# Turning stages 4 to 7 of an RWKV front by DMA instead of by matmul, with the first stages listed in a new order

## The chip, the cores and the metric

The kernel runs on one core of a Trainium2 chip. The metric is the device time of one execution in microseconds (us), as the median of several runs. The engines are called PE (TensorE: matmuls, and beside it PEld, its weight loads), DVE (VectorE), ACT (ScalarE), POOL (GpSimd) and SP (SyncE). POOL also issues the loads that change the number type on the way, SP the plain transfers and the DMA transposes.

## The reference

For batch `b` (4), head `h` (8), and tokens `t` (768) with head size D = 48, a linear attention with a decay per channel is computed, and its output of 3072 tokens by 384 channels goes through a two-layer MLP with a leaky ReLU:

```
for t in range(S):
    cur = einsum('bhd,bhe->bhde', u * k_t, v_t)
    y_t = einsum('bhd,bhde->bhe', r_t, state + cur)
    state = w * state + einsum('bhd,bhe->bhde', k_t, v_t)
...
h = x @ w_in                      # 384 -> 2048
out = maximum(0.01 * h, h) @ w_out   # 2048 -> 384
```

`r`, `k`, `v` and the weights arrive as float32 and are worked on in bfloat16.

## The kernel before, in words

The tokens are cut into 24 **stages** of 128 tokens; stage `n` is chunk `n // 4` of batch `n % 4`. Within a stage the recurrence is a masked product: r is scaled by `w^(t-64)` (table `qtab`), k by `w^(63-t)` (table `ktab`); both scaled tiles are turned, so that channels lie on partitions; their product (128 by 128 tokens for each head) is masked below the diagonal; it multiplies v, and the state carried from the stage four before is added. The diagonal term with `u` comes for stages 0 to 7 (`DIAG`) as a scaled v, and for later stages as a diagonal tile that POOL writes ahead of the mask. The MLP takes the stage's output (`xT`) through `w_in` (four column groups) and `w_out`.

All the instructions are recorded in one list by a small scheduler (`Sched`), which keeps for every buffer its writer and readers and puts semaphore waits where another engine or a transfer is involved. Each engine executes its own instructions strictly in the order of the record, so the order is all that decides who stands behind whom. There are eight PSUM banks, handed out in the order of the record: `take` gives the bank that has been free longest, and the matmul that gets it waits for the last reader of its former content.

The record has two parts. The front (stages 0 to 7, and parts of stages 8 to 13) is written out by hand as a string of steps, `ORDER`; behind it a loop over pairs of stages (`for m in range(FIRST // 2, ...)`) makes the rest by rule. The loop is the same in both kernels. The first step of its first turn, called J3 in the prediction, is eight pairs of `w_in` products for stages 6 and 7 (48 matmuls, line 628).

A step in `ORDER` is a letter and a stage. Those that matter here:

- `k4`, `r4`, `v4`: load of one stage's k, r or v with a cast from float32 to bfloat16 (1024 rows of 48 numbers), issued by POOL (line 223). `k0` and `r0` are plain loads from ACT and SP. `wi2`: one of four groups of `w_in` (line 233). `wo2`: one of four of `w_out` (line 237).
- `P4q`, `P4k`: DVE scales r or k of stage 4 into `qk` (line 353).
- `T4q`, `T4k`: four matmuls with the identity turn it into PSUM (line 407); `t4q`, `t4k`: ACT copies that into `tp` (line 421), or DVE does where an `@` follows (line 419).
- `X8T`: SP issues one DMA transpose that turns r and k of a stage together, from `qk` to `tp` (line 358). `X4` without a `T`: DVE's product of both turned tiles (line 368), for the diagonal term of stages 0 to 7.
- `A`: the eight matmuls of the masked product, into two banks (line 432). `Ma`, `Mb`: DVE masks one bank (line 441, from stage 8 on line 445). `D`: four small matmuls for the diagonal term (line 460). `Q`: the scaled v on DVE (line 375), from stage 8 on two diagonal tiles on POOL (line 393). `q8`: the row sums that these need, three DVE instructions (lines 382 to 386), which read `u_tab`.
- `Y`: the output of a stage on PE (lines 559 and 566), `y`: ACT copies it to `xT` (line 580). `K`: k times v on PE (line 473), `S`: the new state on DVE (line 531, from stage 4 on 534 and 536).
- `G0.2`: 12 matmuls of stage 0 with `w_in` group 2 (line 605), `g0.2`: ACT's leaky ReLU of it (line 615). `J2.5`: six matmuls of twice the width for stages 4 and 5 (line 628), `j2.5` its leaky ReLU (line 638). `H0`: 16 matmuls with `w_out` (line 652), `h0`: ACT's copy and SP's output transfer (lines 664 and 666).
- `F12`: 12 matmuls on ones with no use for their result (line 261), called fillings. `tri`, `id`: mask and identity on POOL. `bc`, `lnw`, `qtab`, `ktab`: the decay tables.
- `u`, `u16`, `U`, `utab`: u is loaded as one row, cast by ACT, spread over the partitions by a matmul with ones, and copied to `u_tab` by ACT (lines 676, 326, 330, 335).

`TURNED` names the first stage that isn't turned by matmul; the front's steps are written to agree with it.

Of the kernel before, what the change touches and what calls it, by code (L numbers as in the profile page):

```python
# [7 lines left out]
AF = mybir.ActivationFunctionType  # L8
AX = mybir.AxisListType
BF16 = mybir.dt.bfloat16  # L10
FP32 = mybir.dt.float32
# [6 lines left out]
HD = H * D  # L18
# [4 lines left out]
NSL = HD // 128  # L23

FIRST, NB, PACE = 6, B, 3
TURNED, DIAG, CARRY, EXACT = 8, 8, 4, 1
ORDER = """
w k0 r0 w8 u8 u wlz tcol k1 ones table one exps qk0 r1 v0z r5 F12 bc wi2 lnw id qtab wu8 v0 id8 u16 F13 Cm P0q ktab U
k3 P1q T0q Wl P0k utab T1q r3 P1k t0q T0k C P5q W T1k t1q@ k4 T5q t0k t1k@ tri t5q F2 A0 X0 v1 X1 F2 A1 M0a F3 D0 wi1
M0b F5 D1 F1 K0 k5 P3k P3q F11 T3k Q0 r4 F3 T3q P4k t3k F3 Y0 M1b v3 t3q T4k M1a y0 F2 K1 A3 r2 t4k Q1 F1 G0.2 M3a wi3  # L30
F1 Y1 S1 g0.2 G0.1 M3b v5 y1 X3 F2 G1.2 r7 P5k g0.1 S0 T5k g1.2 D3 P4q k6 G1.1 Q3 t5k T4q r6 g1.1 K3 P2q Y3 S3 t4q T2q
k2 X5 y3 F2 A5 X4 F1 A4 t2q M5a G3.2 v4 M4b F1 G3.3 wi0 g3.2 M4a D4 D5 G0.3 g3.3 k7 M5b G1.3 P7q g0.3 v7 Q5 K5 P6k G3.1
g1.3 S5 wo2 T6k g3.1 Y5 P6q v2 P2k t6k T6q Q4 y5 r10 F2 K4 T2k t6q@ T7q t2k Y4 v6 t7q@ A6 y4 S4 F1 A2 wo3 G1.0 M6a r11
F1 J2.7 P7k g1.0 M6b wo0 J2.0 j2.7 M2b J2.6 v8 j2.0 X2 M2a J2.2 j2.6 wo1 K7 J2.1 j2.2 v9 S7 K2 J2.4 j2.1 S2 r9 G0.0
P10q j2.4 r8 K6 J2.3 g0.0 S6 v11 D2 G3.0 j2.3 X6 Q2 k8 T7k g3.0 D6 J2.5 Q6 t7k k11 Y2 P11q j2.5 X7 A7 k9 y2 Y6 M7a k10
D7 M7b y6 G2.1 Q7 v10 G2.0 g2.1 G2.3 g2.0 G2.2 g2.3 H1 g2.2 P9q P8q H2 h1 P8k q8 X8T K8 H0 h2 P9k Q8 S8 X9T P10k P11k
K9 X10T H3 h0 q9 X11T S9 Q9 Y7 h3 A9 y7 A8 M8a M9a M9b M8b k12 r12 v12 k13 r13 v13
"""


# [4 lines left out]
class Sched:  # L45
# [7 lines left out]

    def add(self, eng, emit, R=(), W=(), dma=None):
        o = Op()
        o.eng, o.emit, o.dma, o.inc, o.val = eng, emit, dma, False, None
        deps = []
        for key in R:
            w = self.writer.get(key)
            if w is not None:  # L60
                deps.append((w, True))
        for key in W:
            w = self.writer.get(key)
            if w is not None:
                deps.append((w, False))
            for r in self.readers.get(key, ()):
                deps.append((r, False))
        o.deps = []
        for d, raw in deps:
            if d.dma is None and d.eng == eng and dma is None and (eng == "pe" or not raw):  # L70
                continue
            if d is not o and d not in o.deps:
                o.deps.append(d)
        for key in R:
            self.readers.setdefault(key, []).append(o)
        for key in W:
            self.writer[key] = o
            self.readers[key] = []
        self.ops.append(o)
        return o  # L80
# [47 lines left out]
def bass_rwkv5_eagle__then__act_leaky_relu_kernel(  # L128
# [13 lines left out]
    def SB(name, shape, dt=BF16):  # L142
        return ctx.enter_context(nc.sbuf_tensor(name, shape, dt))
# [5 lines left out]
    k_sb = SB("k_sb", [128, NST, HD])  # L149
    v_sb = SB("v_sb", [128, NST, H * E])  # L150
    w_row = SB("w_row", [128, HD // 2], FP32)
    u_row = SB("u_row", [1, HD], FP32)
    one_row = SB("one_row", [128, 128], FP32)
    u_row16 = SB("u_row16", [1, HD])
    w_head = SB("w_head", [H, D], FP32)
    u_head = SB("u_head", [H, D], FP32)
    wu_head = SB("wu_head", [H, D], FP32)
# [3 lines left out]
    lnw = SB("lnw", [128, HD], FP32)  # L161
    u_tab = SB("u_tab", [128, HD])
    k_f = SB("k_f", [128, EXACT, HD], FP32)
    r_f = SB("r_f", [128, EXACT, HD], FP32)
    qtab = SB("qtab", [128, HD])
    ktab = SB("ktab", [128, HD])
    tcol = SB("tcol", [128, 1], FP32)
# [4 lines left out]
    ones = SB("ones", [128, 128])  # L172
# [17 lines left out]
    V, A, PE, SP, G = nc.vector, nc.scalar, nc.tensor, nc.sync, nc.gpsimd  # L190
    sch = Sched(ctx, nc)
    add = sch.add
    free = list(range(8))

    def take():
        i = free.pop(0)
        return ps[i], ("ps", i)

    def give(key):
        free.append(key[1])  # L200

    def dram(h, offset, pattern):
        return bass.AP(tensor=h.tensor, offset=h.offset + offset, ap=pattern)
# [12 lines left out]
    def load_one(n, which, pace=()):  # L216
# [4 lines left out]
        else:  # L221
            dst = {"k": k_sb, "r": r_sb}[which][:, n, :].rearrange("p (h d) -> p h d", d=D)
        add("pool", lambda: G.dma_start(dst, src), R=pace, W=[(which, n)], dma=f"{which}{n}")  # L223

# [12 lines left out]
        add("pool", lambda: G.dma_start(w_out_sb[:, 4 * i:4 * i + 4, :], wout_view[:, 4 * i:4 * i + 4, :]),  # L237
            W=[("wout", i)], dma=f"wout{i}")

    def row(h):  # L240
        return dram(h, 0, [[HD, 1], [1, HD]])

    def by_head(h):
        return dram(h, 0, [[D, H], [1, D]])
# [11 lines left out]
    def fill(n):  # L256
# [6 lines left out]

        add("pe", emit, R=["ones"], W=[("ps", i), f"fill{n}"])

    def identity():
        add("pool", lambda: G.affine_select(ident[:, :], ones[:, 0:128], pattern=[[1, 128]], compare_op=ALU.is_equal,
                                            fill=0.0, base=0, channel_multiplier=-1), R=["ones"], W=["ident"])

# [52 lines left out]
        add("dve", lambda: V.tensor_tensor(wu_head[:, :], w_head[:, :], u_head[:, :], ALU.mult),  # L322
            R=["w_head", "u_head"], W=["wu_head"])

    def u_cast():
        add("act", lambda: A.activation(u_row16[:, :], u_row[:, :], AF.Copy), R=["u_row"], W=["u_row16"])

    def u_spread():
        ps_u, key = u_bank["u"] = take()
        add("pe", lambda: PE.matmul(ps_u[:, 0:HD], ones[0:1, 0:128], u_row16[:, :], start=True, stop=True),  # L330
            R=["ones", "u_row16"], W=[key])

    def u_table():
        ps_u, key = u_bank["u"]
        add("act", lambda: A.activation(u_tab[:, :], ps_u[:, 0:HD], AF.Copy), R=[key], W=["u_tab"])
        give(key)

    u_bank, c_bank = {}, {}
    at_bank, kv_bank, y_bank = {}, {}, {}

    def hd(x):
# [316 lines left out]
    def g2_out(n, c0=0, c1=HD):  # L658
# [14 lines left out]
            W=["w_row"], dma="w"),  # L673
        "w8": lambda: add("sp", lambda: SP.dma_start(w_head[:, :], by_head(w)), W=["w_head"], dma="w8"),
        "u8": lambda: add("sp", lambda: SP.dma_start(u_head[:, :], by_head(u)), W=["u_head"], dma="u8"),
        "u": lambda: add("sp", lambda: SP.dma_start(u_row[:, :], row(u)), W=["u_row"], dma="u"),
        "one": lambda: add("dve", lambda: V.memset(one_row[:, :], 1.0), W=["one_row"]),
        "tcol": tokens, "ones": filled, "exps": exponents, "v0z": zero_v, "qk0": zero_qk, "wlz": zero_w,
        "id": identity, "tri": triangle, "table": preload, "id8": small_identity, "wu8": wu_product,
        "bc": spread_w, "lnw": log_w, "qtab": lambda: table(qtab, qexp, "q"), "ktab": lambda: table(ktab, kexp, "k"),  # L680
        "Cm": columns_mm, "Wl": log_columns, "C": decay_columns, "W": decay_table,
        "u16": u_cast, "U": u_spread, "utab": u_table,
    }
    stage = {
        "P": lambda n, x: prep_half(n, half_of[x]), "T": lambda n, x: turn_mm(n, half_of[x]),
# [108 lines left out]
```

## Time and profile before

| what | before |
|---|---|
| median of 3 runs | 172.35 us (171.53 to 172.49) |
| span of the profiled execution | 168.6 us |
| granted clock of PE | 1.00 of full speed in every stretch |
| PE, DVE, ACT, POOL busy | 163.7, 106.9, 90.8, 103.6 us |
| matmuls | 2170 |
| fillings (line 261) | 69 matmuls |
| DMA transposes | 16, median 2.8 us from issue to landing |

The span runs from the first to the last instruction of the profiled execution; the profile gives no device time of its own for that execution, so the median of the runs stands beside the span, 3.75 us above it. In the views a row has the line of the kernel, the engine, the operation, the tiles (out<-in) and a count; times are us from the span's start. A chain of waits goes back from the last instruction, at each step to what released it.

### The profile page before, as it was taken

The numbers are of one execution on the slowest core, as the hardware profiler recorded it, in microseconds if no ns is written. First come the engines' busy times: TensorE is split into PE (matmuls) and PEld (weight loads), VectorE is DVE, ScalarE is ACT, GpSimd is POOL, SyncE is SP. The second block draws the span as 40 slices with busy tenths as digits, with TensorE's granted clock in tenths as the row PEclk, the third lists the DMA queues.
The fourth block names the chain that finished last, engine by engine and source line by source line (L and its number), as shares of the span: only waits on it lengthen the run. The fifth ranks groups of instructions, "written<-read, shape, count | busy, mean of one in ns | idle before, by whom it ended". The sixth has DMA issues, their size and how long they took to land.

```text
span 168.6 us, 5011 instructions
## 1 busy us (share of the span) xinstructions
PE 163.7 (97%) x2170; PEld 126.1 (75%) x2170; DVE 106.9 (63%) x217; ACT 90.8 (54%) x167; POOL 103.6 (61%) x117
## 2 busy tenths in 40 slices
PE   6899999999999999999999999999999999999994
PEld 4787898988667867867867867768768668668663
DVE  6599799874583999869959959969876050000000
ACT  3837866886123933933834735735637538449221
POOL 7999999990249998994993993993708100000000
PEclk9999999999999999999999999999999999999999
DMA  6999999999999959999599399299241011011012
GB/s 99 142 151 165 170 167 173 182 184 148 130 167 187 163 75 144 155 118 173 71 140 167 64 141 177 71 132 193 59 121 47 0 51 47 0 51 47 29 68 95
DMA packets 99148, 19.67 MB, mean 117 GB/s; under 512 B 92339, under 2 KB 99126, under 8 KB 99126
## 3 DMA queue, kind: packets, MB, share of 16 engines
q0 software_dynamic: 76512, 10.03, 92.1%
q1 hardware_dynamic: 21574, 9.12, 23.2%
q8 instruction: 17, 0.28, 0.7%
q10 hardware_dynamic: 1040, 0.20, 0.6%
q14 instruction: 5, 0.04, 0.1%
HBM read 20.45 MB, written 4.72 MB: 149 GB/s over the span
## 4 chain that ended last, share of the span: by engine, by line
PE 89%; POOL 5%; DMA 4%; issue 0%; ACT 0%; POOLq 0%
PE ps L652 37%; PE ps L628 31%; PE ps L605 6%; PE ps L566 6%; DMA w_in_sb<-in_moe_w_in_dram 4%; PE ps L432 4%; PE ps L473 2%; POOL k_sb L223 2%; POOL r_sb L223 2%; PE ps L407 1%; POOL v_sb L223 1%; PE ps L559 1%; PE ps L261 0%; POOL w_in_sb L233 0%; PE ps L460 0%
## 5 line engine op out<-in xcount | busy, mean ns | idle before, releaser
L652 PE MATMUL ps<-w_out_sb,gT 128*128 128x384 bf16 (+2 forms) x400 | 65.7, 320 | 0.0
L628 PE MATMUL ps<-xT,w_in_sb 128*128 128x256 bf16 x480 | 54.7, 273 | 0.0
L652 PEld LDWEIGHTS ps<-w_out_sb,gT 128*128 128x128 bf16 x400 | 37.9, 98 | 22.0
L393 POOL TENSOR_TENSOR at<-ident,s_tok 128x512 bf16<-128x512 bf16 x32 | 35.0, 1121 | 26.9 <-DVE s_tok L386 26.9
L628 PEld LDWEIGHTS ps<-xT,w_in_sb 128*128 128x128 bf16 x480 | 46.6, 98 | 6.4 <-ACT xT L580 0.2
L638 ACT ACTIVATE gT<-ps 128x512 bf16<-128x512 f32 x80 | 47.8, 597 | 6.4 <-PE ps L628 1.6
L664 ACT ACTIVATE out_sb<-ps 128x384 f32<-128x384 f32 (+2 forms) x25 | 11.9, 478 | 52.9 <-PE ps L652 52.9
L445 DVE CAST_PREDICATED at<-mask,ps 128x512 bf16<-128x512 uint16 x32 | 19.8, 684 | 18.0 <-PE ps L432 18.0
L223 POOL DMA_DIRECT2D v_sb<-in_v_dram x24 | 22.9, 955 | 0.0
L223 POOL DMA_DIRECT2D k_sb<-in_k_dram x23 | 21.5, 965 | 0.4 <-issue 0.4
L223 POOL DMA_DIRECT2D r_sb<-in_r_dram x23 | 21.2, 930 | 0.0
L353 DVE TENSOR_TENSOR qk<-r_sb,qtab 128x384 bf16<-128x384 bf16 x23 | 14.2, 617 | 3.8 <-DMA r_sb<-in_r_dram 3.8
L353 DVE TENSOR_TENSOR qk<-k_sb,ktab 128x384 bf16<-128x384 bf16 x23 | 13.0, 570 | 1.3 <-DMA k_sb<-in_k_dram 1.3
L580 ACT ACTIVATE xT<-ps 128x384 bf16<-128x384 f32 x24 | 11.0, 491 | 4.8 <-PE ps L566 4.8
L605 PE MATMUL ps<-xT,w_in_sb 128*128 128x128 bf16 x192 | 12.5, 219 | 0.4 <-DMA w_in_sb<-in_moe_w_in_dram 0.4
L615 ACT ACTIVATE gT<-ps 128x512 bf16<-128x512 f32 x16 | 9.6, 597 | 5.3 <-PE ps L605 4.9
L605 PEld LDWEIGHTS ps<-xT,w_in_sb 128*128 128x128 bf16 x192 | 11.0, 98 | 0.8 <-DMA w_in_sb<-in_moe_w_in_dram 0.5
L384 DVE TENSOR_TENSOR rku<-r_sb,ku 128x384 bf16<-128x384 bf16 x16 | 10.8, 675 | 0.6
L566 PE MATMUL ps<-at,v_sb 128*32 128x128 bf16 x384 | 10.8, 220 | 0.0
L534 DVE TENSOR_TENSOR sum_t<-ps,st 128x384 bf16<-128x384 f32 x16 | 8.8, 551 | 2.7 <-PE ps L473 2.7
L441 DVE TENSOR_TENSOR at<-ps,mask 128x512 bf16<-128x512 f32 x16 | 10.3, 681 | 0.3 <-PE ps L432 0.3
L261 PE MATMUL ps<-ones 128*128 128x128 bf16 x69 | 8.5, 257 | 1.3 <-DVE ones L251 1.3
(60 smaller groups left out, 135.1 us busy)
## 6 DMA issues: line engine op xcount, KB each, us to landing
out_dram<-out_sb SPq DMA_DIRECT2D x23, 192.0 KB, 3.6
v_sb<-in_v_dram POOLq DMA_DIRECT2D x24, 96.0 KB, 6.3
k_sb<-in_k_dram POOLq DMA_DIRECT2D x23, 96.0 KB, 6.1
r_sb<-in_r_dram POOLq DMA_DIRECT2D x23, 96.0 KB, 5.9
w_in_sb<-in_moe_w_in_dram POOLq DMA_DIRECT2D x4, 384.0 KB, 6.8
w_out_sb<-in_moe_w_out_dram POOLq DMA_DIRECT2D x4, 384.0 KB, 9.3
tp<-qk SPq DMA_TRANSPOSE x16, 2.8
k_f<-in_k_dram ACTq DMA_DIRECT2D x1, 192.0 KB, 2.7
```

The source lines that it names most:

```text
L223: add("pool", lambda: G.dma_start(dst, src), R=pace, W=[(which, n)], dma=f"{which}{n}")
L353: add("dve", lambda: V.tensor_tensor(qk[iq][:, H * half:H * half + H, 0:D], hd(src), hd(tab[:, :]), ALU.mult), R=[(name, n), "qk"[half] + ...
L384: add("dve", lambda: V.tensor_tensor(rku[i2][:, :], r_of(n), ku[i2][:, :], ALU.mult), R=[("r", n), ("ku", i2)], W=[("rku", i2)])
L393: add("pool", lambda hh=hh, s_of=s_of: G.tensor_tensor(at[ia][:, hh, :, :], ident[:, :].unsqueeze(1).to_broadcast([128, NP, 128]), s_of.un ...
L445: add("dve", lambda: V.copy_predicated(at[n % NAT][:, hh, :, :], mask[:, :].bitcast(mybir.dt.uint16).unsqueeze(1).to_broadcast([128, NP, 1 ...
L566: last = PE.matmul(ps_y[32 * q:32 * q + 32, 128 * s:128 * s + 128], a, m, start=not whole and step == 0, stop=step == len(columns[q]) - 1)
L580: add("act", lambda: A.activation(xT[m % NX][:, :, 128 * half:128 * half + 128], ps_y[:, 0:HD].rearrange("p (s t) -> p s t", t=128), AF.Copy),
L605: last = PE.matmul(ps_g[:, 128 * f:128 * f + 128], w_in_sb[:, s, 128 * fb:128 * fb + 128], xT[ix][:, s, t], start=s == 0, stop=s == NSL - 1)
L628: last = PE.matmul(ps_g[:, 256 * f:256 * f + 256], w_in_sb[:, s, 128 * fb:128 * fb + 128], xT[ix][:, s, :], start=s == 0, stop=s == NSL - 1)
L638: add("act", lambda: A.activation(gT[ig][:, 2 * j:2 * j + 2, :].rearrange("p f t -> p (f t)"), ps_g[:, :], AF.Prelu, alpha=0.01), R=[key], ...
L652: last = PE.matmul(ps_o[:, 0:c1 - c0], gT[ig][:, s, 128 * half:128 * half + 128], w_out_sb[:, s, c0:c1], start=s == 0, stop=s == NFB - 1)
L664: add("act", lambda: A.activation(out_sb[io][:, c0:c1], ps_o[:, 0:c1 - c0], AF.Copy), R=[key], W=held)
```

## The change

Stages 4 to 7 are turned by DMA transposes as the later ones were (`X4T` to `X7T`), so their `T` and `t` steps are gone: 32 matmuls, six evictions on ACT and two on DVE. `u_tab` is filled by one casting transfer on POOL's queue that reads the row of u for each of the 128 partitions; the row tile, its cast, its matmul and its eviction are gone. The whole string `ORDER` is new: the order of the loads, of the first stages' steps on every engine, and the places and lengths of the fillings (F15, F8, F12, F16, F26, 77 in all, against 69). The number of products, masks and MLP matmuls is the same. `k12`, `r12`, `v12` and `r13` now stand ahead of POOL's diagonal tiles `Q8` and `Q9`, and `v13`, `k13` and `v11` between or behind them.

```
-TURNED, DIAG, CARRY, EXACT = 8, 8, 4, 1
+TURNED, DIAG, CARRY, EXACT = 4, 8, 4, 1
 ORDER = """
-w k0 r0 w8 u8 u wlz tcol k1 ones table one exps qk0 r1 v0z r5 F12 bc wi2 lnw id qtab wu8 v0 id8 u16 F13 Cm P0q ktab U
-k3 P1q T0q Wl P0k utab T1q r3 P1k t0q T0k C P5q W T1k t1q@ k4 T5q t0k t1k@ tri t5q F2 A0 X0 v1 X1 F2 A1 M0a F3 D0 wi1
-M0b F5 D1 F1 K0 k5 P3k P3q F11 T3k Q0 r4 F3 T3q P4k t3k F3 Y0 M1b v3 t3q T4k M1a y0 F2 K1 A3 r2 t4k Q1 F1 G0.2 M3a wi3
...
-P10q j2.4 r8 K6 J2.3 g0.0 S6 v11 D2 G3.0 j2.3 X6 Q2 k8 T7k g3.0 D6 J2.5 Q6 t7k k11 Y2 P11q j2.5 X7 A7 k9 y2 Y6 M7a k10
-D7 M7b y6 G2.1 Q7 v10 G2.0 g2.1 G2.3 g2.0 G2.2 g2.3 H1 g2.2 P9q P8q H2 h1 P8k q8 X8T K8 H0 h2 P9k Q8 S8 X9T P10k P11k
-K9 X10T H3 h0 q9 X11T S9 Q9 Y7 h3 A9 y7 A8 M8a M9a M9b M8b k12 r12 v12 k13 r13 v13
+tcol exps w r0 ones wlz r1 w8 u8 k1 k0 one v0z id wi0 r3 tri table F15 bc lnw k3 qtab ktab qk0 wu8 id8 F8 Cm v0 P1q P0q T1q T0q k2 P1k T1k P0k T0k
+t1q@ Wl C t1k@ X1 F12 A1 M1b r2 v1 t0k t0q X0 D1 P3q v3 P3k wi1 A0 M0a M0b F16 T3q T3k D0 Q0 P2k F26 T2k W t3k M1a P2q Y0 t3q A3 K1 Q1 T2q X3 k4 t2k
+y0 t2q v2 Y1 M3a G0.0 M3b D3 Q3 A2 r4 y1 G1.0 Y3 X2 D2 M2a G0.1 wi3 y3 G1.1 K3 M2b g1.0 Q2 P4q P4k G3.1 Y2 g0.0 K2 y2 S2 S1 X4T G3.0 g3.0 g0.1 G2.1 k5
+g1.1 G3.3 g3.3 G0.3 g0.3 g3.1 S3 g2.1 G2.0 P5k A4 r5 P5q X5T G2.3 g2.3 K0 wi2 X4 D4 M4a G1.3 g1.3 v4 G3.2 S0 M4b K4 v5 K5 Q4 g2.0 X5 A5 r7 M5a G0.2
+M5b D5 Q5 k7 Y4 y4 G1.2 Y5 g1.2 G2.2 P7k v7 K7 P7q y5 J2.5 J2.1 wo2 S5 S7 X7T J2.7 j2.5 g0.2 S4 wo3 J2.2 wo1 wo0 j2.7 k6 r6 X7 g3.2 k9 g2.2 J2.0 D7 A7
+Q7 M7a M7b r9 j2.1 P6q k8 P6k P9k j2.2 P8k J2.3 J2.6 X6T J2.4 j2.4 j2.3 P9q r8 X6 P8q u Y7 q8 q9 j2.0 v8 H3 H2 v6 X9T H0 D6 X8T Q6 r11 K8 h3 P11q v10
+r10 A6 j2.6 H1 M6b r13 M6a S8 v12 v9 Y6 k10 y7 h2 K9 h0 P10k k12 y6 A8 r12 k11 P10q S9 Q8 h1 v13 M8b P11k Q9 A9 X11T M9b K6 M9a k13 X10T M8a S6 v11
 """
...
-    def row(h):
-        return dram(h, 0, [[HD, 1], [1, HD]])
+    def rows(h):
+        return dram(h, 0, [[0, 128], [1, HD]])
...
+    def load_u():
+        add("pool", lambda: G.dma_start(u_tab[:, :], rows(u)), W=["u_tab"], dma="u")
...
-        "u": lambda: add("sp", lambda: SP.dma_start(u_row[:, :], row(u)), W=["u_row"], dma="u"),
+        "u": load_u,
...
-        "u16": u_cast, "U": u_spread, "utab": u_table,
```

More of the change, by code (lines that the diff above doesn't have):

```diff
@@ L25 @@
 FIRST, NB, PACE = 6, B, 3
-TURNED, DIAG, CARRY, EXACT = 8, 8, 4, 1
+TURNED, DIAG, CARRY, EXACT = 4, 8, 4, 1
 ORDER = """
-w k0 r0 w8 u8 u wlz tcol k1 ones table one exps qk0 r1 v0z r5 F12 bc wi2 lnw id qtab wu8 v0 id8 u16 F13 Cm P0q ktab U
-k3 P1q T0q Wl P0k utab T1q r3 P1k t0q T0k C P5q W T1k t1q@ k4 T5q t0k t1k@ tri t5q F2 A0 X0 v1 X1 F2 A1 M0a F3 D0 wi1
-M0b F5 D1 F1 K0 k5 P3k P3q F11 T3k Q0 r4 F3 T3q P4k t3k F3 Y0 M1b v3 t3q T4k M1a y0 F2 K1 A3 r2 t4k Q1 F1 G0.2 M3a wi3
[L31 to L34, printed above, removed]
-P10q j2.4 r8 K6 J2.3 g0.0 S6 v11 D2 G3.0 j2.3 X6 Q2 k8 T7k g3.0 D6 J2.5 Q6 t7k k11 Y2 P11q j2.5 X7 A7 k9 y2 Y6 M7a k10
-D7 M7b y6 G2.1 Q7 v10 G2.0 g2.1 G2.3 g2.0 G2.2 g2.3 H1 g2.2 P9q P8q H2 h1 P8k q8 X8T K8 H0 h2 P9k Q8 S8 X9T P10k P11k
-K9 X10T H3 h0 q9 X11T S9 Q9 Y7 h3 A9 y7 A8 M8a M9a M9b M8b k12 r12 v12 k13 r13 v13
+tcol exps w r0 ones wlz r1 w8 u8 k1 k0 one v0z id wi0 r3 tri table F15 bc lnw k3 qtab ktab qk0 wu8 id8 F8 Cm v0 P1q P0q T1q T0q k2 P1k T1k P0k T0k
[5 more added lines that the diff above has]
+r10 A6 j2.6 H1 M6b r13 M6a S8 v12 v9 Y6 k10 y7 h2 K9 h0 P10k k12 y6 A8 r12 k11 P10q S9 Q8 h1 v13 M8b P11k Q9 A9 X11T M9b K6 M9a k13 X10T M8a S6 v11
 """
@@ L151, in bass_rwkv5_eagle__then__act_leaky_relu_kernel @@
     w_row = SB("w_row", [128, HD // 2], FP32)
-    u_row = SB("u_row", [1, HD], FP32)
     one_row = SB("one_row", [128, 128], FP32)
-    u_row16 = SB("u_row16", [1, HD])
     w_head = SB("w_head", [H, D], FP32)
@@ L323, in wu_product @@
             R=["w_head", "u_head"], W=["wu_head"])
[L325 to L338, printed above, removed]
+    def load_u():
+        add("pool", lambda: G.dma_start(u_tab[:, :], rows(u)), W=["u_tab"], dma="u")
+    c_bank = {}
     at_bank, kv_bank, y_bank = {}, {}, {}
```

## The prediction

> **What bounds the kernel now.** I read the page's shares first, then the chain of waits in order of time, then the DMA queues.
>
> ```profile
> span 168.6 us, 5011 instructions
> PE 163.7 (97%) x2170; PEld 126.1 (75%) x2170; DVE 106.9 (63%) x217; ACT 90.8 (54%) x167; POOL 103.6 (61%) x117
> DMA  6999999999999959999599399299241011011012
> q0 software_dynamic: 76512, 10.03, 92.1%
> PE 89%; POOL 5%; DMA 4%; issue 0%; ACT 0%; POOLq 0%
> ```
>
> TensorE (PE) is the bound: 97% busy and 89% of the chain. The other 9% of the chain is the load queue (POOL and DMA), and it lies at the front; there the DMA row stands at 9 as well, slice after slice, until about 59 us (14 slices of 4.2 us). So there are two resources with no room in the front, and the end is set by whichever is later. The chain of waits gives the marks:
>
> ```profile
> 9.86 6.43 DMA w_in_sb<-in_moe_w_in_dram
> 16.29 0.05 issue
> 16.34 0.84 PE ps L605 x12
> ...
> 18.26 0.69 PE ps L605 x12
> 18.95 0.22 PE ps L407 x4
> 19.18 0.17 PE ps L473 x4
> 19.35 0.17 PE ps L559 x3
> 19.52 0.34 PE ps L566 x16
> ...
> 53.36 5.41 PE ps L628 x48
> 58.77 2.60 PE ps L652 x16
> ```
>
> From 16.34 on every piece is PE. J3, the first step of the loop that is the same in both kernels (48 matmuls at L628), starts at 53.36 and ends at 58.77; behind it PE goes on without a gap. So the question is when J3 ends in the changed kernel: the loop behind it adds the same time, and has no room to give a loss back.
>
> **The change, PE alone.** The first matmul of the MLP (G0) and the fillings:
>
> ```profile
> 10.37 0.40 PE L432 MATMUL ps<-tp 48*128 48x128 bf16 x8
> ...
> 11.59 0.78 PE L261 MATMUL ps<-ones 128*128 128x128 bf16 x11
> 12.20 0.39 PE L407 MATMUL ps<-ident,qk 128*128 128x128 bf16 x4
> ...
> 14.59 0.83 PE L605 MATMUL ps<-xT,w_in_sb 128*128 128x128 bf16 x12
> ```
>
> A filling costs 0.055 us (11 from 11.59 to 12.20), a turn by matmul 0.22, a K 0.17, a Y without state 0.17+0.34 = 0.51. Between G0 and J3 PE loses: six of the eight turns that stood there (stages 4 to 7), 1.32; the two turns of stage 2 and Y1, which now stand ahead of G0, 0.44+0.51; 11 fillings, 0.6 (none is left there); the wait of 16.34 for a w_in group that landed at 16.29, 0.35, since the changed PE order has more work ahead of that group. It gains K0, 0.17. Sum: 3.05 less.
>
> G0 itself comes later, because VectorE (DVE) now scales stages 3 and 2 ahead of the masks that Y0 and Y1 need:
>
> ```profile
> 12.35 0.55 DVE L375 TENSOR_TENSOR vs<-v_sb,ps 128x384 bf16<-128x384 bf16 x1
> 12.81 0.35 DVE L353 TENSOR_TENSOR qk<-k_sb,ktab 128x384 bf16<-128x384 bf16 x1
> 13.08 1.28 DVE L441 TENSOR_TENSOR at<-ps,mask 128x512 bf16<-128x512 f32 x2
> 14.28 0.54 DVE L375 TENSOR_TENSOR vs<-v_sb,ps 128x384 bf16<-128x384 bf16 x1
> ```
>
> By starts, a mask costs 0.60, a scaling 0.27, a v product 0.46; a diagonal product I put at 0.34. A1 can end at 10.4 (the row at 10.37 is before's second A; after's first stands behind 12 slow fillings). From there DVE has four masks, four scalings, two v products and one diagonal product until Q1: 2.4+1.1+0.92+0.34 = 4.8, so 15.2; Y1 and its waits bring G0 to about 16.0 (15.3 to 16.5), 1.4 later than 14.59. PE alone: 1.4 - 3.05 = **-1.6 us** (-2.3 to -1.1); J3 would start at 51.75.
>
> What else goes costs nothing either way. The evictions of the turns (ScalarE has six, DVE two) were beside PE. Of u's table the cast, one matmul and an eviction go, all ahead of 9 us, where PE has fillings. The eight more fillings stand ahead of G0, where PE waits for DVE anyway; without that cover they cost 8 x 0.055 = 0.4.
>
> **The change, the transfers.** Four stages' turns join two others (8 and 9), all six now inside the stretch in which loads queue up; before, the first turn was issued at 44.9 with the loads all but through. On SP they stand in the order 4, 5, 7, 6, 9, 8, ahead of four output transfers. What a turn takes, alone and beside loads:
>
> ```profile
> L358 SPq DMA_TRANSPOSE tp<-qk x2: 1231/1234/1238, 83.2 to 84.6; - x2
> ...
> DMA to landing us min/median/max: 2.7/4.3/5.9
> ```
>
> Of two, the one alone landed in 2.7 us and the one beside loads in 5.9. On PE, A4, A5 and A7 wait for such landings. Stage 4's scaling waits for r of stage 4, POOL's 14th transfer; before's 14th, a load issued at 13.2, landed 6.1 us later:
>
> ```profile
> DMA to landing us min/median/max: 6.1/6.1/6.1
> ```
>
> That is 19.3; two scalings and what DVE has ahead of them put the turn's issue at about 20.2. PE reaches A4 ten groups (0.69 each), two Y, an A, two K and two small products after 16.0, at about 24.9. With 5.9 us the turn lands at 26.1, a wait of about 1; the next two by the same walk 0.4 to 1 each. Everything behind these matmuls on PE waits too. That alone would use up the 1.6.
>
> The larger cost falls on the loads. What the engines moved with a turn alone, with loads alone, and with both:
>
> ```profile
> 49.50:50.50 1.00, 1.00 (x8) 0.61 (x7) 0.94 (x2) 0.35 (x1) 0.93 (x1) 1.00 1.16 260
> 57.00:58.00 1.00, 1.00 (x12) 0.90 (x10) 0.97 (x3) 0.94 (x2) 0.77 (x2) 1.00 2.67 141
> 64.00:66.50 2.50, 2.50 (x20) 1.71 (x19) 2.43 (x6) 0.49 (x1) 2.50 (x4) 1.00 1.75 149
> ```
>
> (the last number is GB/s). A turn moves 256 KB (128 x 1024 bf16): 1.0 us at 260. A load of 96 KB takes 0.70 at 141. In the third stretch both moved 149 x 2.5 = 372 KB; with 258 of the turn, 114 are left for the loads, 0.8 us of work alone, so a turn kept the loads back 2.5 - 0.8 = 1.7 us. The loads' landings (us from issue) say the same:
>
> ```profile
> DMA to landing us min/median/max: 4.6/4.9/5.2
> ```
> ```profile
> DMA to landing us min/median/max: 5.0/6.6/7.0
> ```
>
> The first row has the six loads issued from 51.68 to 56.08, the second the six from 84.06 to 88.46, which run into a turn (and an output): 1.7 more at the median. A turn costs the loads 1.0 (bytes alone) to 1.7; I take 1.4, as the second view has an output in it.
>
> [...]
>
> Whom a late load holds: in DVE's new order the scaling of k's stage 11 stands ahead of three of the four masks of stages 8 and 9 and of S6, and J3's pairs 4 to 7 take the PSUM banks that these read. k of stage 11 is the 46th transfer on POOL's queue (37 loads, 8 weights, u). The last of before's 42 front transfers:
>
> ```profile
> L223 POOL DMA_DIRECT2D v_sb<-in_v_dram x1: 1117/1117/1117, 36.8 to 36.8; - x1
> ...
> DMA to landing us min/median/max: 9.5/9.6/9.8
> ```
>
> It landed at 36.8 + 9.5 = 46.3; a queue that takes 9.5 us to land is bound by the DMA engines, not by POOL's issuing. Three more loads (2.1) and u (128 rows of 1.5 KB; nothing to a load's 0.7, I take 0.5) make 48.9 to 49.0. Six turns at 1.4 add 8.4; outputs of 192 KB that come into the stretch add 0 to 2 (0.7 each; I take 1.0). So k of stage 11 lands at **58.4** (55.0 to 61.2). Behind it, in DVE's order:
>
> ```profile
> 53.43 2.48 DVE L445 CAST_PREDICATED at<-mask,ps 128x512 bf16<-128x512 uint16 x4 [2.60 <-PE ps L432]
> ...
> 65.33 0.55 DVE L534 TENSOR_TENSOR sum_t<-ps,st 128x384 bf16<-128x384 f32 x1
> 65.91 0.36 DVE L536 TENSOR_TENSOR st<-sum_t,wl 128x384 bf16<-128x384 bf16 x1
> ```
>
> the scaling 0.3, three masks 1.8, S6 0.9, then J3's last pair 0.7: 3.7, with waits 3.8. J3 ends at 62.2 (58.8 to 65.0) instead of 58.77: **+3.4 us** (0.0 to +6.2). The turn waits on PE lie inside this. v of stage 9, which K9 waits for ahead of J3, is four transfers earlier and gives the same within 0.5. POOL's two diagonal tiles of stage 8 and 9, now ahead of v13, k13 and v11, wait for u and k: v11 lands at about 62, its K11 stands at about 65, so nothing. The loop's own loads start up to 5 us later and are wanted some 20 us after landing.
>
> The sum is made on the span of 168.6; the runs' median of 172.35 is 3.75 above it, which I leave as it is: 172.35 + 3.4 = 175.7.
>
> **Rivals.**
>
> *The turns hide (faster).* If k of stage 11 lands by 53.4, no bank is late (pair 4 at 51.75 + 4 x 0.66 wants the mask by 54.4, which is 0.9 behind the landing), and PE's -1.6 stands: 170.8. That leaves 53.4 - 49.0 = 4.4 us for six turns, 0.7 each. For it: PE is the chain's 89%, and a turn's bytes may fit in the engines' gaps. Against it: 1.0 by bytes alone, and the queue's 9.5 us show no gaps. It is also what comes if my count of the queue is 2 us too high and outputs stay out.
>
> *The waits on PE alone.* If the loads are kept back just 1.0 per turn and no output meets them, J3 ends at 58.8, as before: 172.4. What PE saves, the waits of A4, A5, A7 and the banks take: within 0.5%.
>
> *The full price.* 1.7 for each turn and two outputs: J3 ends at 65.0, 178.6; the first turn's issue took 2.71 us against 1.24 for later ones, and among queued loads it may be longer still.
>
> ```profile
> 44.92 2.71 SPq L358 DMA_TRANSPOSE tp<-qk  x1
> ```
>
> **How the numbers follow.** Forecast, with the full price as its upper end (173.3 to 178.6): 0.63. Parity: 0.14. Turns hidden: 0.23. "Within 0.5%" is 0.86 us, about what a measurement of this kernel can tell from no change. The predicted time is the likeliest case's, 175.7. The range takes in part of the faster case at its centre and reaches the full price: 170.8 to 178.6.
>
> **What would show it.** Right: PE idle in the first stretch at A4 and A5 with a DMA landing named, PE waiting inside J3's pairs for DVE's masks, these behind k of stage 11 landing near 58; six turns landing in 5 to 6 us; J3's end near 62 and the loop behind it as long as before. Wrong: G0 far from 16.0; k of stage 11 before 54; a gap later in the loop (POOL's tiles or the stage 10 and 11 turns, which stand behind the outputs on SP), which I put at nothing.

## The result, and the profile after

| | before | after |
|---|---|---|
| median of 4 runs each, on one chip | 172.42 us (171.53 to 172.77) | 186.62 us (184.98 to 187.47) |
| span of the profiled execution | 168.6 | 183.1 |
| J3 starts, ends | 53.36, 58.77 | 67.22, 73.18 |
| PE's mean granted clock | 1.00 | 0.97 |

The changed kernel takes 1.085 times as long (95% interval 1.078 to 1.092): 14.2 us more, where +3.4 was forecast, and 8 us above the end of the range. The time of a run stands 1.7 to 2.0 us above its span wherever both are known, so the two profiled executions were quicker than the medians, by 1.6 us after (184.98) and an estimated 2 before (some 170.4).

Line numbers differ in the changed kernel: L590 is G, L613 J, L637 H, L417 A, L445 D, L544 and L551 Y, L458 K, L392 a turn by matmul; on DVE L338 is a scaling, L353 the product `X`, L426 and L430 masks, L360 `Q`, L369 and L371 steps of `q8`; L343 is SP's DMA transpose, L218 a load, L378 POOL's diagonal tile.

The page of the changed kernel's profile, its shares and its chain by engine:

```profile
span 183.1 us, 4954 instructions
PE 166.8 (91%) x2145; PEld 128.2 (70%) x2145; DVE 109.3 (60%) x215; ACT 85.2 (47%) x159; POOL 104.0 (57%) x118
PE 74%; DMA 14%; DVE 9%; ACT 1%; issue 1%; POOL 0%; POOLq 0%
```

PE is as busy as before in microseconds (166.8 against 163.7), but 16.3 us of the span pass without it, where 4.9 did. On the chain the load queue's 9% at the front is gone, and 14% DMA and 9% DVE have come in the middle. The chain in order of time (start, us, what) says which DMA:

```profile
16.49 0.78 PE ps L590 x12
...
19.15 1.36 PE ps L590 x24
...
24.21 10.74 DMA tp<-qk
...
37.84 7.21 DMA tp<-qk
45.05 0.02 issue
45.08 0.43 DVE prod L353
...
48.23 7.54 DMA tp<-qk
55.78 0.02 issue
55.80 0.42 DVE prod L353
...
60.20 3.03 DVE qk L338
63.24 1.21 DVE at L426 x2
...
67.22 5.96 PE ps L613 x48
```

Three turns, of stages 5, 7 and 6, stand on the chain one behind the other with 25.5 us together. Those of 7 and 6 can't start earlier in this order: a turn is issued when DVE has scaled its stage, and these scalings stand on DVE behind the product (L353) of the turn before, which waits until that has landed. The waits for the turns of stages 7 and 6, on DVE:

```profile
45.08 0.42 DVE L353 TENSOR_TENSOR prod<-tp 128x512 bf16<-128x512 bf16 x1 [3.80 <-DMA tp<-qk]
...
55.80 0.42 DVE L353 TENSOR_TENSOR prod<-tp 128x512 bf16<-128x512 bf16 x1 [6.79 <-DMA tp<-qk]
```

No load is on the chain behind G0.

PE's timeline, its only waits between G0 and J3 (in brackets the idle time before the row, and what ended it):

```profile
28.29 0.61 PE L417 MATMUL ps<-tp 48*128 48x128 bf16 x8 [2.81 <-DMA tp<-qk]
...
35.09 0.40 PE L417 MATMUL ps<-tp 48*128 48x128 bf16 x8 [1.16 <-DMA tp<-qk]
```
```profile
45.65 0.24 PE L445 MATMUL ps<-wu,prod 128*128 128x2 bf16 x4 [2.94 <-DVE prod L353]
```
```profile
64.49 0.34 PE L544 MATMUL ps<-ident,vs 128*128 128x128 bf16 x3 [4.32 <-DVE at L426]
```

These are A4, A5, D7 and Y6: 11.2 us. The first three wait for a turn, at once or through DVE's product. The last waits for the masks of stage 6. The turn of stage 6 landed at 55.78, but its masks began only at 63.2: between them DVE has the row sums for the diagonals of stages 8 and 9 and a scaling (`P11q`) that took 3.12 instead of 0.35 (the last section shows it). So this wait is as much of DVE's order as of the turn.

The stretch from G0 to J3 and the one behind it, by windows (length, then busy time and count of PE, PEld, DVE, ACT, POOL, PE's granted clock, DMA share, GB/s), first before, then after:

```profile
14.60:53.36 38.76, 38.35 (x641) 31.15 (x642) 28.48 (x65) 22.33 (x42) 29.20 (x34) 1.00 1.83 167
53.36:168.60 115.24, 112.95 (x1368) 84.94 (x1368) 67.30 (x118) 59.98 (x109) 60.84 (x63) 1.00 0.89 97
```
```profile
16.50:67.22 50.72, 39.49 (x583) 31.58 (x584) 28.37 (x58) 17.77 (x36) 31.42 (x37) 0.91 1.78 151
67.22:183.10 115.88, 113.50 (x1369) 85.22 (x1366) 68.36 (x121) 59.98 (x109) 57.16 (x58) 0.99 0.79 94
```

From J3 on both kernels take the same (115.9 and 115.2). So the loss of 14.5 us in span is all in the front, and in these two executions it splits so: G0 1.9 later; 58 matmuls fewer, 2.7 by the prediction's prices, and before's wait of 0.35 gone; 11.2 of waits; and 39.49 of PE work where 38.35 - 2.7 = 35.65 should stand, 3.8 more, which goes with PE's clock, 0.91 in the mean. 1.9 - 2.7 - 0.35 + 11.2 + 3.8 = 13.9, which is J3's delay. J3 itself is 0.55 longer, for the clock as well (0.89 over its 5.96 us). The terms are not independent: work that the low clock stretches fills time in which PE would else have waited.

### The profile page after: what moved, and what is told of

It is laid out like the page before. It is cut to its first block, busy times and chain, and to the rows that moved or that the text cites. A ratio compares the mean times of both kernels' runs of the same rounds, so it can differ in the third digit from the quotient of the medians.

```text
span 183.1 us, 4954 instructions
## 1 busy us (share of the span) xinstructions
PE 166.8 (91%) x2145; PEld 128.2 (70%) x2145; DVE 109.3 (60%) x215; ACT 85.2 (47%) x159; POOL 104.0 (57%) x118
## 3 DMA queue, kind: packets, MB, share of 16 engines
q10 hardware_dynamic: 1040, 0.20, 0.5%
## 4 chain that ended last, share of the span: by engine, by line
PE 74%; DMA 14%; DVE 9%; ACT 1%; issue 1%; POOL 0%; POOLq 0%
PE ps L637 29%; PE ps L613 26%; DMA tp<-qk 14%; PE ps L551 5%; PE ps L417 4%; PE ps L256 3%; DVE qk L338 3%; PE ps L458 2%; DVE at L426 2%; PE ps L590 2%; PE ps L392 2%; DVE vs L360 1%; DVE rku L369 1%; DVE st L516 1%; PE ps L296 1%
## 5 line engine op out<-in xcount | busy, mean ns | idle before, releaser
L637 PE MATMUL ps<-w_out_sb,gT 128*128 128x384 bf16 (+2 forms) x400 | 65.6, 320 | 0.0
L613 PE MATMUL ps<-xT,w_in_sb 128*128 128x256 bf16 x480 | 55.0, 275 | 0.0
L378 POOL TENSOR_TENSOR at<-ident,s_tok 128x512 bf16<-128x512 bf16 x32 | 35.0, 1120 | 34.5 <-DVE s_tok L371 34.5
L637 PEld LDWEIGHTS ps<-w_out_sb,gT 128*128 128x128 bf16 x400 | 37.9, 98 | 22.4
L623 ACT ACTIVATE gT<-ps 128x512 bf16<-128x512 f32 x80 | 47.5, 598 | 12.5 <-PE ps L613 8.0
L613 PEld LDWEIGHTS ps<-xT,w_in_sb 128*128 128x128 bf16 x480 | 47.2, 99 | 6.7
L430 DVE CAST_PREDICATED at<-mask,ps 128x512 bf16<-128x512 uint16 x32 | 19.9, 683 | 15.4 <-PE ps L417 15.4
L218 POOL DMA_DIRECT2D k_sb<-in_k_dram x23 | 21.4, 929 | 4.8 <-issue 4.8
L218 POOL DMA_DIRECT2D r_sb<-in_r_dram x23 | 21.6, 949 | 1.9 <-issue 1.9
L218 POOL DMA_DIRECT2D v_sb<-in_v_dram x24 | 22.3, 949 | 0.0
L338 DVE TENSOR_TENSOR qk<-r_sb,qtab 128x384 bf16<-128x384 bf16 x23 | 17.5, 762 | 0.0
L590 PE MATMUL ps<-xT,w_in_sb 128*128 128x128 bf16 x192 | 14.2, 237 | 0.0
L353 DVE TENSOR_TENSOR prod<-tp 128x512 bf16<-128x512 bf16 x8 | 3.4, 421 | 17.3 <-DMA tp<-qk 17.3
L590 PEld LDWEIGHTS ps<-xT,w_in_sb 128*128 128x128 bf16 x192 | 12.5, 107 | 0.7 <-issue 0.2
L338 DVE TENSOR_TENSOR qk<-k_sb,ktab 128x384 bf16<-128x384 bf16 x23 | 12.9, 568 | 0.0
L417 PE MATMUL ps<-tp 48*128 48x128 bf16 x192 | 9.0, 232 | 4.0 <-DMA tp<-qk 4.0
L369 DVE TENSOR_TENSOR rku<-r_sb,ku 128x384 bf16<-128x384 bf16 x16 | 11.6, 722 | 0.6
L426 DVE TENSOR_TENSOR at<-ps,mask 128x512 bf16<-128x512 f32 x16 | 10.4, 682 | 1.5 <-PE ps L417 1.4
L600 ACT ACTIVATE gT<-ps 128x512 bf16<-128x512 f32 x16 | 8.6, 598 | 5.7 <-PE ps L590 5.7
L417 PEld LDWEIGHTS ps<-tp 48*128 48x128 bf16 x192 | 6.0, 100 | 7.1 <-issue 6.7
```

Of the source, the lines that this page charges most:

```text
L338: add("dve", lambda: V.tensor_tensor(qk[iq][:, H * half:H * half + H, 0:D], hd(src), hd(tab[:, :]), ALU.mult), R=[(name, n), "qk"[half] + ...
L369: add("dve", lambda: V.tensor_tensor(rku[i2][:, :], r_of(n), ku[i2][:, :], ALU.mult), R=[("r", n), ("ku", i2)], W=[("rku", i2)])
L378: add("pool", lambda hh=hh, s_of=s_of: G.tensor_tensor(at[ia][:, hh, :, :], ident[:, :].unsqueeze(1).to_broadcast([128, NP, 128]), s_of.un ...
L417: last = PE.matmul(at_bank[n][hh][0][:, 128 * p:128 * p + 128], tp[it][rows, NP + p, :], tp[it][rows, p, :], start=True, stop=True)
L426: add("dve", lambda: V.tensor_tensor(at[n % NAT][:, hh, :, :], part, mask[:, :].unsqueeze(1).to_broadcast([128, NP, 128]), ALU.mult), R=[a ...
L430: add("dve", lambda: V.copy_predicated(at[n % NAT][:, hh, :, :], mask[:, :].bitcast(mybir.dt.uint16).unsqueeze(1).to_broadcast([128, NP, 1 ...
```

## The experiments

Theory after the result: the turns are late where PE and DVE wait for them in a row, and they land late because of the loads queued beside them (the front's six landed 5.7 to 10.7 us after issue, one alone in before 2.7). Rivals: the new order does it without the turns; or the loads that the turns keep back are what costs, whether or not anyone waits for a turn; or the clock. Ratios below are to the kernel before, measured beside each experiment on the same chip, with 95% intervals.

**1. The new order without the DMA turns.** The changed kernel, stages 4 to 7 turned by matmul at the same places.

```
-... S1 X4T G3.0 ...
+... S1 T4q T4k t4q t4k G3.0 ...
```

X5T, X6T and X7T are replaced alike.

> The changed kernel, with stages 4 to 7 turned by matmul again (T and t steps at the places of the four DMA transposes); order, loads, u's table and fillings as changed. Theory (turns by DMA among queued loads land 7 to 11 us after issue, and four such waits in series hold PE): the four waits go, about 172.5 us (171 to 174), J3 starts at 52 to 54. Rival (the new order itself is bad: G0 late, row sums ahead of stage 6's masks on DVE): 180 us or more, PE still idle ahead of Y6.

173.38 against 172.24 us: 1.008 (1.004 to 1.013). J3 starts at:

```profile
55.63 5.24 PE ps L614 x48
```

The time is inside what was expected, J3's start 1.6 us behind it. PE has no wait before Y6, though DVE's order is the changed one. The rest of the change (order, loads, fillings, u's table) costs 1.1 us; the DMA turns cost the other 13.

**2. The DMA turns without the new order.** The kernel before, with `T` and `t` of stages 4 to 7 taken out and `XnT` put behind the second scaling of its stage, as for stage 4:

```
-... D3 P4q k6 G1.1 Q3 t5k T4q r6 ... S3 t4q T2q ...
+... D3 P4q X4T k6 G1.1 Q3 r6 ... S3 T2q ...
```

> The kernel before, with only stages 4 to 7 turned by DMA transposes (issued behind their second scaling). Theory: stage 6's and 7's turns meet w_out's packets, land about 10 us after issue, and PE waits for them: 180 to 184 us. Rival (the order is to blame): at most 174 us.

191.97 against 172.24: 1.117 (1.109 to 1.124). PE's waits, all for landings:

```profile
26.48 0.61 PE L430 MATMUL ps<-tp 48*128 48x128 bf16 x8 [5.42 <-DMA tp<-qk]
31.13 0.61 PE L430 MATMUL ps<-tp 48*128 48x128 bf16 x8 [3.83 <-DMA tp<-qk]
...
46.04 0.61 PE L430 MATMUL ps<-tp 48*128 48x128 bf16 x8 [6.90 <-DMA tp<-qk]
```

The loss is 8 us above the range expected. The turns are the cause in either order, and the new order makes their price smaller, 13 instead of 20 us. It has more PE work between a turn and its reader: PE came to A4 5.0 us behind the issue of stage 4's turn (20.50 to 25.48), here to A5 2.4 us behind that of stage 5's (18.64 to 21.06). That this is the whole difference was not tested.

**3. Turns that nobody waits for.** This and the next two ask what the turns do to the loads alone. The kernel before keeps its matmul turns, and SP issues four DMA transposes more, of the same tiles, into spare tiles that nobody reads.

```
+    def bystander(n):
+        add("sp", lambda: SP.dma_start_transpose(spare[n - 4][...], qk[iq][...]), ...)
 ORDER: + B4, B5, B6, B7, each behind the second P of its stage
```

> The kernel before, turning by matmul as before, with four more DMA transposes of stages 4 to 7 into spare tiles that nothing reads, so that they burden the queues and nobody waits for them. Theory (the waits for the landings are the loss): within 1% of before, 172 to 174 us, though the transposes land 7 to 11 us after issue. Rival (the step on record: loads kept back by each transpose 1.4 us set the end): loads 5 us or more later, 175 us or more.

181.55 against 172.46: 1.056 (1.049 to 1.062). My theory failed here: 9 us without a single wait for a turn. The last load of the front, issued at 36.9 as in before (where it landed 9.5 us later):

```profile
DMA to landing us min/median/max: 19.8/19.8/19.9
```

It landed 10.3 us later than in before: 2.6 for each turn. The price is good to some tenths: in before an output and the turn of stage 8 were issued 1.9 and 1.5 us ahead of that landing (44.50 and 44.92), here 0.8 and 0.4 us ahead. On the chain a load stands where PE stood:

```profile
25.08 18.65 DMA v_sb<-in_v_dram
...
43.87 0.33 PE ps L478 x4
```

The K on L478 idles 4.20 us for that v.

**4. The same bystanders beside the new order.** Experiment 1 with the four extra transposes at the places of `X4T` to `X7T`:

```
-... S1 T4q T4k t4q t4k G3.0 ...
+... S1 B4 T4q T4k t4q t4k G3.0 ...
```

> The changed kernel with matmul turns for stages 4 to 7 (as in the first experiment, 173.4 us), and four more DMA transposes of those stages into spare tiles that nothing reads, at the places where the changed kernel has its own. It parts the loss of 13 us in two. Theory (PE's waits for the turns' landings are most of it): 174.5 to 178 us, since this order has its loads early enough. Rival (the loads that the transposes keep back are most of it): 182 us or more.

181.08 against 171.03: 1.056 (1.047 to 1.066), between the two expectations. Against experiment 1 (1.008) the load traffic alone costs 1.056 / 1.008 = 1.048, about 8 us; the changed kernel stands another 1.085 / 1.056 = 1.027, about 5 us, above it. The chain again has one load in the middle, 20.2 us under way, and no turn:

```profile
25.52 20.23 DMA r_sb<-in_r_dram
...
46.19 1.04 PE ps L400 x8
```

The two parts don't simply add: in the changed kernel no wait for a load is left on the chain, so what the loads lose must lie beside the waits for turns there. That is inferred, not tested.

**5. Plain copies in place of the extra transposes.** Experiment 3 with four plain copies of the same bytes, in rows of 2 KB, and, in a last run, cut into pieces of 256 bytes, since by the pages' packet counts a transpose has 1056 packets (experiment 3 has 4224 more than before), a 2 KB copy 144, and the cut copy 1040.

```
-SP.dma_start_transpose(spare[n - 4][:, :, :], qk[iq]...)
+SP.dma_start(spare[n - 4]..., qk[iq]...)              # 2 KB rows
+SP.dma_start(spare[n - 4][:, :, 0:128], qk[iq]...)    # 8 pieces of 256 bytes in a row
```

> The kernel before with four plain copies of the same bytes (qk to a spare tile, 128 rows of 2 KB) in place of the four transposes that nobody waits for (181.6 us there, the last front load landing at 56.6 instead of 46.4, 2.6 us each). [...] Rival (the bytes count): 2.6 us each again, 181 us.

> The kernel before with four plain copies of the same bytes at the places where the matmul turns of stages 4 to 7 have their tiles ready, this time cut into 8 pieces of 256 bytes in each row, so 1024 packets a copy (the transposes had 1056, the copies in 2 KB rows 144). Nobody reads the copies. If the number of packets is what keeps the loads back, these copies are as dear as transposes: the last front load lands 8 to 11 us later than its 46.4 (it was 56.6 beside four transposes), and the time is 178 to 182. If the transposing itself is dear and packets are not, the last front load lands at 49 to 50 as beside the copies in 2 KB rows (49.4), and the time is 172 to 174.

In 2 KB rows 172.66 against 171.03: 1.008 (1.005 to 1.012); in 256-byte pieces 176.36 against 170.70: 1.031 (1.023 to 1.038). The last load of the front, first beside the one, then beside the other:

```profile
DMA to landing us min/median/max: 12.6/12.6/12.7
```
```profile
DMA to landing us min/median/max: 16.3/16.4/16.5
```

For 256 KB each the loads are kept back by (12.6 - 9.5) / 4 = 0.8 us, (16.4 - 9.5) / 4 = 1.7, and 2.6 as a transpose. The copies in 2 KB rows cost less than the 173 to 176 us expected, and both expectations of the last run were missed: the cutting into small packets costs 0.9, the transposing another 0.9. The three parts are about equal, as far as prices good to some tenths can tell; bytes in long rows are a third of a transpose's price.

**6. One turn alone.** The kernel before with stage 7 alone turned by DMA.

```
-... t6q@ T7q t2k Y4 v6 t7q@ A6 ... P7k g1.0 ... k8 T7k g3.0 ... Q6 t7k k11 ...
+... t6q@ t2k Y4 v6 A6 ... P7k X7T g1.0 ... k8 g3.0 ... Q6 k11 ...
```

> The kernel before with stage 7 alone turned by a DMA transpose, which is the one with the most time between its scaling (29.5) and its first use (37.3). Theory: it lands 8 to 10 us after issue, PE waits 1 to 2.5 us for it and saves 0.4: 173.5 to 175.5 us. Rival (one turn alone hides): 172 us, no change or slightly faster.

174.00 against 171.03: 1.014 (1.007 to 1.021). The turn lands in 10.1 us, A7 waits for it:

```profile
41.22 0.40 PE L430 MATMUL ps<-tp 48*128 48x128 bf16 x8 [1.76 <-DMA tp<-qk]
```

The last front load lands 12.4 us after its issue instead of 9.5: 2.9 for one turn. So even one did not pay. But the trace accounts for only a part of the 3.0 us: in this execution G0 starts late, long before the turn's issue at 31.0,

```profile
17.26 0.83 PE L603 MATMUL ps<-xT,w_in_sb 128*128 128x128 bf16 x12
```

and from G0 to J3 it is 40.0 us (17.26 to 57.29) against 38.8 in before (14.59 to 53.36), 1.3 more, which is A7's 1.76 less the two matmul turns that are gone (0.44). G0 varies so between executions of the same steps (the figures are in the section on the prediction); where it stands in the runs that weren't profiled isn't known.

**7. Loads out of the turns' way.** In the changed kernel POOL holds the loads from `v7` on until the turn of stage 5 has landed (a wait of `v7` on that turn); or the four loads of `w_out` move behind `k6 r6`.

```
-"v": lambda n, x: load_one(n, "v"),
+"v": lambda n, x: load_one(n, "v", [("tp", 5, 0)] if n == 7 else ()),
```
```
-... J2.1 wo2 S5 ... S4 wo3 J2.2 wo1 wo0 j2.7 k6 r6 X7 ...
+... J2.1 S5 ... S4 J2.2 j2.7 k6 r6 wo2 wo3 wo1 wo0 X7 ...
```

> The changed kernel, but POOL issues v of stage 7 and all behind it only once stage 5's transpose has landed, so that this transpose meets no w_out packets. Theory (a transpose's landing is set by the packets queued beside it): stage 5's lands in 5 to 6.5 us instead of 10.7, PE reaches J3 about 4 us earlier, 180 to 185 us in all, although the loads behind start 8 us later. Rival (transposes in the front are slow in themselves, by their issue on SP): landing 10 us again, and with the later loads 187 us or more.

> The changed kernel with the four w_out loads moved behind k and r of stage 6 on POOL's queue, so that stage 5's transpose shares the engines with small load packets instead of w_out's large ones. [...] Rival (only the bytes or the count of queued transfers matter): 10 us again, 186.6 us.

Held: 184.84 against 172.24, 1.075 (1.068 to 1.082). The turn of stage 5 lands in 6.9 instead of 10.7, and PE doesn't wait at A5; but the loads come later and meet the next turn (9.0 instead of 7.2), and D7 waits 4.74 instead of 2.94. The time is inside the theory's range, but J3 starts at 68.28, 1.1 later than in the changed kernel's profile where 4 earlier was expected. Moved: 181.51, 1.056 (1.049 to 1.063), a larger gain than the expected 183 to 184 us and the largest of any edit that keeps the turns, with the same turn at

```profile
DMA to landing us min/median/max: 8.2/8.2/8.2
```

and J3 at 64.00. The landing of stage 5's turn depends on what loads stand beside it, and the wait moves to the next turn. But loads don't explain every landing: with the loads held, stage 4's turn took 9.1 us instead of 7.7, beside fewer of them, and A4 waited 4.30 instead of 2.81. Why isn't known.

**8. DVE's queue behind the turn of stage 6.** The diagonals of stages 8 and 9 and `P11q` go behind the masks of stage 6 on DVE; then the same with the `w_out` loads moved as in 7.

```
-... Y7 q8 q9 j2.0 ... K8 h3 P11q v10 ... M6b r13 M6a S8 ...
+... Y7 j2.0 ... K8 h3 v10 ... M6b r13 M6a q8 q9 P11q S8 ...
```

> The changed kernel, with stage 6's masks ahead of the two row sums and r's scaling of stage 11 on DVE. Theory (behind stage 6's late turn, DVE's order adds a wait of its own, PE idle 4.3 us ahead of Y6): Y6 starts when H1 ends, J3 at about 63.2 (then stage 8's turn, landing at 62.3, holds A8), 182 to 184 us. Rival (only the turn's landing counts): PE waits just as long for A8, 186 us.

> The changed kernel with both moves: w_out's loads behind k and r of stage 6, and stage 6's masks first on DVE. Theory: both gains add up where they don't cover each other; J3 at about 62, 179 to 180 us, still 7 us slower than before since A4, A5 and D7 wait for landings. Rival: no better than the better one of the two, 181.5 us.

First: 184.86 against 172.46, 1.073 (1.067 to 1.080); the wait of 4.32 before Y6 is gone, but two others of 2.0 each come, before A8 and inside J3's pairs, each for a step S that DVE now does late. The time is just above the 182 to 184 expected. With both edits: 186.44, 1.082 (1.075 to 1.090), worse than the `w_out` edit alone, with 1.95 idle inside J3 and 42 of its matmuls at a low clock (0.50 from 65 to 70 us, 0.82 from 70 to 75):

```profile
66.97 7.12 PE L613 MATMUL ps<-xT,w_in_sb 128*128 128x256 bf16 x42 [1.95 <-DVE sum_t L519]
```

Gains of such edits don't add; the second expectation was missed by 6 us.

**9. The clock.** Fillings into the four waits: F50 ahead of A4, F26 ahead of A5, F52 ahead of D7, F78 ahead of Y6.

```
-... P5k A4 ... X5 A5 ... J2.0 D7 A7 ... v9 Y6 ...
+... P5k F50 A4 ... X5 F26 A5 ... J2.0 F52 D7 A7 ... v9 F78 Y6 ...
```

> The changed kernel with fillings ahead of A4 (50), A5 (26), D7 (52) and Y6 (78), as long as PE's idle times there. Theory (the waits are for landings, and PE's lower granted clock behind an idle time costs time only behind the last wait): clock back to 1.00, J3's 48 matmuls take 5.24 us instead of 5.96, 185.3 us (184.5 to 186). Rival (the lower clock is a main part of the loss): 182 us or less.

189.25 against 172.46: 1.099 (1.092 to 1.105), 2.6 us longer than the changed kernel instead of a little shorter. The clock stood at 1.00 from 25 to 35 us and J3 took 5.24, but the last filling had to wait for a bank that DVE's masks read, and so came behind the wait, on the path:

```profile
64.63 6.00 PE L257 MATMUL ps<-ones 128*128 128x128 bf16 x78 [4.04 <-DVE at L427]
```

So the low clock is a term of the loss (3.8 + 0.55 us) that follows from the waits, not their cause, and these fillings don't win it back. Without the 6.00 us of the last one J3 would have started at an estimated 66.4 (72.41 - 6.00), 0.8 ahead of the changed kernel: most of what a full clock saves comes back as waiting. A5, for one, waited 2.24 instead of 1.16. Fillings at the first three places alone were not tried.

## Why the prediction was wrong, step by step

- **What bounds the kernel**: right. Two full resources in the front, and no room in the loop to win a loss back (115.9 against 115.2 us from J3 on).
- **G0 at 16.0 (15.3 to 16.5), 1.4 later than 14.59**: 16.49, and 16.0 to 16.6 in the seven other profiled executions of the new order up to G0, so the walk through DVE's queue held. The 14.59 that it was compared with did not: the five profiled executions with before's steps up to G0 (before and experiments 3, 5 and 6) have 14.6, 14.7, 15.9, 16.7 and 17.3. The one on which the forecast stands was the earliest, and that the new order makes G0 later at all is not shown. Of the 3.75 us between before's span and its median, which the sum left as it was, only 1.7 to 2.0 is what a time has over its own span.
- **PE alone -1.6**: the count was right (58 matmuls fewer between G0 and J3, as 24 + 8 + 19 + 11 - 4 says), the size not quite. Experiment 1 has J3 2.27 later with eight turns (1.76) and 0.93 us without a matmul between G0 and J3: 2.27 - 1.76 - 0.93 = -0.4. G0 accounts for 0.5 of the missing 1.2; the rest was not found.
- **"With 5.9 us the turn lands at 26.1"**: mis-sized. The issue came at 20.50 against my 20.2, the landing 7.7 us later; over the front

```profile
L343 SPq DMA_TRANSPOSE tp<-qk x6: 1240/1331/3141, 20.5 to 56.5; - x6
...
DMA to landing us min/median/max: 5.7/7.6/10.7
```

The 5.9 was from a turn of the loop, beside a few loads. In the front 8, 10, 17, 13, 10 and 4 of POOL's loads were under way when the six turns were issued.
- **"The turn waits on PE lie inside this"**: this is the step that failed. I let J3's end follow from one late load, and counted the waits of A4, A5 and A7 as covered by it. They are a chain of their own: the issues of the turns of stages 7 and 6 stand behind DVE's product of the turn before, so a late landing delays the next issue too. I forecast 1 + 0.4 to 1 + 0.4 to 1 of waits and nothing at stage 6; measured were 2.81, 1.16, 2.94 and 4.32 (the last in part for DVE's order). With the same extra transposes and nobody waiting for them the kernel is 5 us faster (experiment 4); the turns cost 13 us in all (experiment 1). That the landings stand end to end is read from the trace; no run takes DVE's products out from between them.
- **"A turn costs the loads 1.0 to 1.7; I take 1.4"**: mis-sized by nearly half. 2.6 (experiment 3) and 2.9 (6). I divided bytes by GB/s; by experiment 5 bytes in long rows are 0.8 of the 2.6. And of the stretch from 64.0 to 66.5, from which the 1.7 came, I gave to the loads all that wasn't the turn's, though an output issued at 63.47 was under way in it too. At 2.6 for each of six turns the prediction's own sum would have given 7.2 more, an estimated 183, so this term alone leaves the range too. The number of packets counts beside the bytes: the same 256 KB cost 0.8 in 144 packets and 1.7 in 1040. But 1.7 against 2.6 at nearly the same number of packets (1040 and 1056) says that it is not the whole price; what the rest is, no run shows.
- **k of stage 11 at 58.4 (55.0 to 61.2)**: it was issued at 46.5 and landed 13.2 us later, at 59.8,

```profile
L218 POOL DMA_DIRECT2D k_sb<-in_k_dram x1: 883/883/883, 46.5 to 46.5; - x1
...
DMA to landing us min/median/max: 13.2/13.3/13.4
```

  inside the range by luck. Five turns had landed ahead of it; if they alone kept it back, they cost 2.2 each, (59.8 - 49.0) / 5. The sixth was issued 3.2 us before that landing and three outputs in its last 2 us, in place of six at 1.4 and an output. And nobody waited: J3 started 7.4 us behind that landing, and its pairs had no wait for a bank in the changed kernel.
- **The rivals**: turns that hide (170.8) and parity (172.4) needed a price of 0.7 to 1.0 for a turn. The full price (178.6) took the loads alone to their upper bound; no rival had the turns' own chain as what ends last.
- **The loop's later gaps at nothing**: right.

## What to carry to other kernels

When a matmul is exchanged for a transfer, ask first whether the consumer's issue order makes the landings a chain: one engine in order between two transfers puts their latencies end to end, as the 10.7, 7.2 and 7.5 us here. Size a transfer's latency and what it takes from others at a place with the same queue, and count its packets and its kind as well as its bytes (the same 256 KB kept the loads back 0.8 us in 144 packets, 1.7 in 1040 and 2.6 as a transpose of 1056). A copy that nobody reads, added to the kernel as it is, prices what it takes from others in one run. Before reading a shift of 1 or 2 us off two profiles, see how far the same steps move between executions of one kernel.

## What the runs showed of the hardware that was not expected

- PE's clock. After 2.81 us idle (until 28.29) it ran at half speed in the 5 us of this window; windows as above:

```profile
28.00:33.00 5.00, 4.71 (x52) 4.54 (x53) 2.73 (x5) 1.55 (x3) 5.00 (x7) 0.50 1.49 165
...
```
```profile
45.00:47.00 2.00, 1.35 (x20) 1.18 (x21) 1.50 (x4) 0.00 (x0) 1.34 (x2) 1.00 2.67 142
```

  After 2.94 us idle (until 45.65) it ran on at 1.00. Idle times of nearly the same length had different outcomes, and what decides isn't shown: in experiment 8's first kernel 2.20 us idle (until 27.81) were followed by a clock of 0.55 from 28.5 to 32.0 (24 of the `w_in` matmuls took 2.72 us from 29.27 on, and 1.50 at 19.14), while in experiment 7's second 2.79 us, until the same time, left it at 1.00 (24 took 1.50 at 29.10).
- A DVE operation beside POOL's diagonal tile: a scaling of the same shape took 0.35 at 56.14 and 3.12 at 60.12, and ended at 63.24, just behind POOL's two tiles:

```profile
56.14 0.35 DVE L338 TENSOR_TENSOR qk<-r_sb,qtab 128x384 bf16<-128x384 bf16 x1
...
60.12 3.12 DVE L338 TENSOR_TENSOR qk<-r_sb,qtab 128x384 bf16<-128x384 bf16 x1
```
```profile
60.96 2.05 POOL L378 TENSOR_TENSOR at<-ident,s_tok 128x512 bf16<-128x512 bf16 x2
```

  In experiment 8's first kernel another DVE operation, of 0.36 us elsewhere, took 2.47 beside the same two tiles (63.26 to 65.73, the tiles 63.44 to 65.50). Nothing in the kernel's semaphores ties the two. What they have in common is the end: both DVE operations ended 0.2 us behind the tiles. The scaling's record starts 0.84 us ahead of them, which the rows don't explain, and by what a POOL tile would hold DVE up was not tried.
- POOL's issue of a load stalled three times (2.56, 2.22 and 1.55 us, around 40 to 46 us, with nothing named) while loads took up to 20 us to land. The last two stalls ended at 43.23 and 45.66, each 0.3 us behind the landing of an older load (issued at 24.65 and 25.52, 18.2 and 19.8 us under way). What POOL waited for was not tried.
